# Spectral products over both parts in one pass, layer-norm sums taken while PSUM is emptied, and seven-product blocks in two more units

## The chip, the cores and the metric

The kernel runs on one core of one Trainium2 chip. The metric is the device time of one execution in microseconds (us); lower is better. One core has a matrix engine (TensorE; PE in the profile, with its weight loads as PEld), a vector engine (VectorE, DVE), a scalar engine (ScalarE, ACT), a general engine (GpSimd, POOL), and a queue engine (SyncE, SP) from which most DMA transfers are issued. Each engine takes its instructions in the order in which they were written, and waits where an operand is not ready or a buffer is still read.

## The reference, cut to what matters

Two layers of the same kind are applied to a sequence of S = 2048 tokens with D = 512 channels, in bf16. Each layer is a long convolution with gating and then a feed-forward network with F = 1792:

```python
def _A_ref(q, k, v, shift_k, ssm_k, ssm_D):
    kv = causal_shift_conv(k, shift_k) * v          # 4 taps
    y = irfft(rfft(pad(kv)) * rfft(pad(ssm_k)))[:S] # convolution along the sequence
    return q * (y + kv * ssm_D)
def _B_ref(x, w_gate, w_up, w_down):
    return (silu(x @ w_gate) * (x @ w_up)) @ w_down
x = A_q
x = x + _A_ref(_layernorm(x), A_k, A_v, ...)   # layer 0
x = x + _B_ref(_layernorm(x), ...)
x = x + _A_ref(_layernorm(x), A_k, A_v, ...)   # layer 1, same k, v, filters
x = x + _B_ref(_layernorm(x), ...)
```

Mean and variance of a layer norm run over the 512 channels of a token, with an epsilon of 1e-5. The convolution result does not depend on x, so it is computed once and used by both layers.

## The kernel before, in words

**Tiling.** The sequence is cut into four blocks c of 512 tokens, each held as 128 partitions by R = 4 rows by 512 channels. The convolution is done by blocks in the frequency domain: for every block the values X (from `kv`) and the filter H are transformed by matmuls with cosine and sine tables (`fwd`) and sums and differences on DVE (`m`, then X or H), the spectra are multiplied (`product`, which makes or adds to Z from X and G, where G is the spectrum of the filter), and Z is turned back by matmuls with `inv` (`inverse`) into Yk. A spectrum has four slots and two parts (real and imaginary), 512 channels each: 4096 elements per partition. Block c of the result needs the products of all pairs of blocks that sum to it, so Z is written by a first product and added to by later ones.

**Feed-forward units.** The network is done in 16 units (layer, c, h), each of two rows of a block (HP = 2, so 256 tokens). Their order is (0,0,0), (0,0,1), (1,0,0), (1,0,1), (0,1,0), (0,1,1), (1,1,0), (1,1,1), (0,2,0) and so on to (1,3,1). `prologue` (L926) stands ahead of each unit: the layer norm of x, the gate with Yk (`n`, then `xc<-xc,n`), the layer norm in front of the network, the normalised rows z, and their transposition by DMA into zT. `ffn` (L1085) takes the 14 tiles of F in groups of 4, 4, 4 and 2 (`GROUPS`). The gate and up products go to PSUM tiles pf; ACT applies silu (sg) and copies the up half (ht, hr); DVE multiplies. Units with ROWWISE groups (`by_rows`, L1060) have tokens on the partitions, so that `hr` has to be transposed by DMA into sg before the down product; their pf matmuls are 512 wide. The other groups have F on the partitions and 256-wide pf matmuls. The down product (L1159) is 512 wide, into the two PSUM tiles pd; ACT copies pd to dn (L1201), and DVE adds dn to x (L1204).

**Seven products.** In the units listed in `STRASSEN` (L31) the down product of a pair of F tiles, two token rows and two halves of D is done as a 2 x 2 block product with seven 256-wide matmuls instead of four of 512 (`seven`, L1004). That needs sums of weight blocks (wsa, wsb, wsc; `weight_sums`, L981, five passes of 1792 elements on DVE, once), sums and differences of the activations (cb, L1013 to L1017, three DVE operations for each group), four PSUM tiles per unit (two of the ring pd, two of pc), four copies out of PSUM on ACT (mt, L1046) and five sums on DVE (L1051 to L1058). Before, this is so for all groups of (0,3,0), (0,3,1), (1,3,0) and for two groups of (1,3,1).

**Statistics.** `ln_stats` (L851) takes mean and variance on DVE by `bn_stats` (L856) and `bn_aggr` (L857), adds epsilon (ve, L859), and has POOL take the power -1/2 (rstd, L861). `ln_stats_act` (L867) does it on ACT: a sum (jk with accumulation), a mean (nm), a sum of squares (jk, L881), ve (L885), and the same power on POOL (L887). `ST1` and `ST2` choose, for the first and the second layer norm, which units take which.

**Order.** Every operation is first recorded in a `Plan` by `add` with an engine, a cost and a delay; `Plan.order` (L200) then emits them in the sequence given by the table `ORDER`, a permutation of the recorded operations that was fixed ahead. Costs and delays decide which slot of a ring a buffer gets, and so what waits for what, but the sequence of instructions on each engine, SP's DMA issues among them, is that of the table. Buffers come from rings of fixed size: pf has four PSUM banks, pc and pd two each; s8 (ten slots of 8 KB per partition) holds spectra and larger intermediates, t4 (two slots of 4 KB) the partial products of `product`.

Of the kernel before, what the change touches and what calls it, by code (L numbers as in the profile page):

```python
# [9 lines left out]
P = 128  # L10
F32 = mybir.dt.float32
# [9 lines left out]
ST1 = lambda l, c, h: (l, c, h) in {(0, 0, 0), (0, 1, 0), (0, 2, 0), (0, 3, 0), (1, 0, 0)}  # L21
# [9 lines left out]
STRASSEN = {(0, 3, 0): 4, (0, 3, 1): 4, (1, 3, 0): 4, (1, 3, 1): 2}  # L31
# [88 lines left out]
]  # L120
R = 4

# [1346 lines left out]
```

## Time and profile before

| | before |
|---|---|
| median of 3 runs (lowest, highest) | 340.92 us (340.49, 341.29) |
| the profiled execution: its own time | 340.95 us |
| its span (first to last work on the engines) | 339.2 us |
| granted TensorE clock, mean | 0.998 |
| PE busy | 332.2 us, 98% |
| DVE busy | 305.4 us, 90% |
| ACT busy | 257.8 us, 76% |
| POOL busy | 41.1 us, 12% |

Times inside the profile are microseconds from the start of the span. A group line gives the line of the kernel, engine, operation, output and inputs by name and shape, the count, then the busy time of the group and the mean nanoseconds of one, then the idle time of that engine just before the group's instructions and what ended it. Consecutive matmuls overlap, so that the mean duration of one is longer than the distance from one start to the next.

### The profile page before, as it was taken

What the parts mean: (1) busy time and instruction counts of PE and PEld (TensorE: products, weight loads), DVE (VectorE), ACT (ScalarE), POOL (GpSimd) and SP (SyncE); (2) the same over time, 40 slices, a digit from 0 to 9 for tenths busy, and PEclk for the clock granted to TensorE, in tenths of its full rate; (3) what the DMA queues carried; (4) which work ended last, traced back from release to release, by engine and by line L of the source; (5) the groups of instructions that cost most, each with busy time, mean ns of one, the idle gap of its engine ahead of it and who ended that gap; (6) DMA issues with size and microseconds to landing.
All of it is one profiled execution on the core that took longest, in us unless ns stands there. A gap on an engine that the chain in (4) does not pass through costs nothing.

```text
span 339.2 us, 5867 instructions
## 1 busy us (share of the span) xinstructions
PE 332.2 (98%) x2119; PEld 201.9 (60%) x2151; DVE 305.4 (90%) x552; ACT 257.8 (76%) x514; POOL 41.1 (12%) x46
## 2 busy tenths in 40 slices
PE   8999999999999999999999999999999999999996
PEld 6647864644454564654445555645445487867884
DVE  7999999999999999999999999999999866987464
ACT  6899999988987467877899994869575465657463
POOL 4010110303110400103010200111201000100000
PEclk9999999999999999999999999999999999999999
DMA  7999403312643458341323245431414140213201
GB/s 287 322 312 354 59 15 79 62 31 48 140 108 77 98 123 161 75 111 31 63 48 77 46 80 129 115 37 32 89 11 94 28 92 2 49 47 73 55 0 64
DMA packets 77992, 31.59 MB, mean 93 GB/s; under 512 B 69765, under 2 KB 75786, under 8 KB 77962
## 3 DMA queue, kind: packets, MB, share of 16 engines
q1 hardware_dynamic: 77808, 31.13, 39.5%
q8 instruction: 17, 0.28, 0.4%
q14 instruction: 13, 0.11, 0.1%
q10 hardware_dynamic: 154, 0.07, 0.1%
HBM read 12.33 MB, written 2.10 MB: 43 GB/s over the span
## 4 chain that ended last, share of the span: by engine, by line
PE 83%; ACT 6%; DVE 5%; DMA 4%; issue 1%; POOL 1%; SPq 0%; ACTq 0%
PE pf L358 51%; PE pd L1159 18%; PE ps L358 6%; PE ps L1034 6%; DMA zT<-z 2%; DMA kn<-in_A_k_dram 1%; PE ps L844 1%; ACT H L466 1%; ACT X L466 1%; PE ps L505 1%; DVE bnst L856 1%; DVE m L587 1%; ACT jk L881 1%; ACT jk L875 1%; ACT hs L534 1%
## 5 line engine op out<-in xcount | busy, mean ns | idle before, releaser
L358 PEld LDWEIGHTS <-zT 128*128 128x128 bf16 x528 | 51.4, 98 | 61.1 <-DMA zT<-z 1.4
L358 PE MATMUL pf<-wu_sb,zT 128*128 128x512 bf16 x258 | 64.8, 379 | 0.4
L358 PE MATMUL pf<-wg_sb,zT 128*128 128x512 bf16 x256 | 63.6, 379 | 0.6 <-DMA zT<-z 0.3
L1159 PE MATMUL pd<-wd_sb,sg 128*128 128x512 bf16 x217 | 53.4, 379 | 0.5 <-DMA sg<-hr 0.2
L861 POOL TENSOR_TENSOR rstd<-ve,nhalf 128x2 f32<-128x2 f32 x24 | 27.9, 1165 | 206.4 <-DVE ve L859 206.4
L1072 ACT ACTIVATE sg<-pf 128x512 bf16<-128x512 f32 x66 | 38.9, 605 | 11.9 <-PE pf L358 11.4
L1073 ACT CAST hr<-pf 128x512 bf16<-128x512 f32 x66 | 38.5, 591 | 11.8 <-PE pf L358 11.0
L358 PE MATMUL pf<-zT,wg_sb 128*128 128x256 bf16 x368 | 46.7, 273 | 0.1
L358 PE MATMUL pf<-zT,wu_sb 128*128 128x256 bf16 x368 | 45.9, 273 | 0.0
L358 PEld LDWEIGHTS <-wg_sb 128*128 128x128 bf16 x368 | 35.9, 98 | 8.4
L358 PEld LDWEIGHTS <-wu_sb 128*128 128x128 bf16 x368 | 36.0, 98 | 7.3
L1159 PEld LDWEIGHTS <-sg 128*128 128x128 bf16 x224 | 21.7, 98 | 24.2 <-DMA sg<-hr 0.9
L1132 ACT ACTIVATE sg<-pf 128x512 bf16<-128x512 f32 x46 | 27.5, 608 | 8.1 <-PE pf L358 8.0
L856 DVE BATCH_NORM_STATS2 bnst<-xc 128x6 f32<-128x512 bf16 x48 | 31.4, 684 | 0.5
L1136 ACT CAST ht<-pf 128x512 bf16<-128x512 f32 x46 | 26.7, 591 | 5.7 <-PE pf L358 5.5
L1159 PE MATMUL pd<-wd_sb,ht 128*128 128x512 bf16 (+1 forms) x125 | 30.2, 369 | 0.3
L1139 DVE TENSOR_TENSOR ht<-ht,sg 128x512 bf16<-128x512 bf16 (+1 forms) x31 | 16.9, 548 | 8.5 <-ACT ht L1136 5.0
L700 DVE TENSOR_TENSOR t<-X,G 128x2048 bf16<-128x2048 bf16 x18 | 21.9, 1217 | 0.0
L704 DVE TENSOR_TENSOR t<-X,G 128x2048 bf16<-128x2048 bf16 x18 | 21.9, 1217 | 0.0
L1201 ACT CAST dn<-pd 128x512 bf16<-128x512 f32 x24 | 14.1, 594 | 10.2 <-PE pd L1159 7.6
L466 ACT ACTIVATE X<-ps 128x512 bf16<-128x512 f32 x32 | 19.1, 613 | 3.5 <-PE ps L358 3.1
L1079 DVE TENSOR_TENSOR hr<-hr,sg 128x1024 bf16<-128x1024 bf16 x27 | 18.5, 685 | 2.4 <-ACT hr L1073 1.6
(139 smaller groups left out, 506.8 us busy)
## 6 DMA issues: line engine op xcount, KB each, us to landing
hn<-in_A_ssm_k_dram SPq DMA_DIRECT2D x4, 512.0 KB, 3.9
vt<-in_A_v_dram SPq DMA_DIRECT2D x4, 512.0 KB, 6.5
xc<-in_A_q_dram SPq DMA_DIRECT2D x4, 512.0 KB, 6.2
out_dram<-xc SPq DMA_DIRECT2D x15, 128.0 KB, 1.8
wg_sb<-in_B_w_gate_dram SPq DMA_DIRECT2D x1, 1792.0 KB
wu_sb<-in_B_w_up_dram SPq DMA_DIRECT2D x1, 1792.0 KB, 7.5
wd_sb<-in_B_w_down_dram SPq DMA_DIRECT2D x1, 1280.0 KB, 11.2
sg<-hr SPq DMA_TRANSPOSE x66, 2.5
```

The costliest lines, as they stand in the source:

```text
L358: nc.tensor.matmul(o, lhsT=lhsT, rhs=rhs, start=(n == 0), stop=(n == len(terms) - 1))
L466: add("ACT", act(D), lambda: nc.scalar.activation(out=view(), in_=ps.t[:], func=ACT.Copy, scale=scale), r=[ps], w=[(buf, keys)], conv=conv)
L700: dve(n * D, lambda t1=t1, part=part: nc.vector.tensor_mul(out=t1.t[:], in0=x.t[:, sl, 0, :], in1=g.t[:, sl, part, :]), [(x, key(slots, (0 ...
L704: dve(n * D, lambda t2=t2, part=part: nc.vector.tensor_mul(out=t2.t[:], in0=x.t[:, sl, 1, :], in1=g.t[:, sl, 1 - part, :]), [(x, key(slots ...
L856: add("DVE", 0.6, lambda st=st, i=i: nc.vector.bn_stats(out=st.t[:], in_=xs[c].t[:, i, :]), r=[(xs[c], (i,))], w=[st])
L861: add("POOL", pw, lambda: nc.gpsimd.tensor_tensor(out=rstd.t[:], in0=ve.t[:], in1=nhalf.t[:].to_broadcast((P, n)), op=ALU.pow), r=[ve, nha ...
L1034: nc.tensor.matmul(bank.t[:, half_ * C:(half_ + 1) * C], lhsT=lhsT(i), rhs=rhs(i), start=(first and i == 0 and half_ == 0), stop=(last and ...
L1072: add("ACT", act(D), lambda ps=ps, dst=dst, o=o, which=which: nc.scalar.activation(out=rows(dst, o), in_=ps.t[:], func=ACT.Silu) if which ...
L1073: out=rows(dst, o), in_=ps.t[:], func=ACT.Silu) if which == "g" else nc.scalar.copy(out=rows(dst, o), in_=ps.t[:]),
L1132: add("ACT", act(D), lambda ps=ps, o=o, sg=sg: nc.scalar.activation(out=sg.t[:, o:o + 2, :], in_=ps.t[:], func=ACT.Silu), r=[ps], w=[(sg, ...
L1136: add("ACT", act(D), lambda ps=ps, o=o, ht=ht: nc.scalar.copy(out=ht.t[:, o:o + 2, :], in_=ps.t[:]), r=[ps], w=[(ht, (o // 2,))], due=(uni ...
L1159: nc.tensor.matmul((pds[o] if not cs.start else pds[HP]).t[:, cs], lhsT=ht.tiles(q, o), rhs=wt["d"].t[:, ft, cs], start=(ft == std0 and no ...
```

## The change

1. `product`: instead of a pass for each part (two multiplications of 2048 elements, one combination, and where Z exists an addition, for each of the two parts), X of one part is multiplied with both parts of G at once: two multiplications of 4096 elements, in which one operand is read with a repeated (stride 0) middle dimension; two combinations of 2048; and where Z exists one addition of 4096. The partial products t1 and t2 lie in s8 (eleven slots now); the ring t4 is gone.
2. Statistics: for the layer-1 norm of (1,1,0), (1,1,1), (1,2,0) and (1,2,1) the row sums come from ACT with the copy out of pd (`accum_out` on dn), added to the known mean of x from the norm before (`means`), and the squares from ACT; `bn_stats` and `bn_aggr` go away there. (1,0,0), whose sums ACT took in two passes of its own, gets them at the copy in the same way. In the other units epsilon is brought in by a constant triple (0, 0, 512 eps) that `bn_aggr` reads as a further set of statistics, so that the DVE operation for ve (L859) is gone and POOL reads the variance from mv itself.
3. `STRASSEN` has two more units, (1,2,0) and (1,2,1), all four groups; `weight_sums` is recorded ahead of (1,2,0).
4. X and Yk of block 3 use the PSUM ring pf instead of pc; the load of `w_down` is issued with its smaller part first; some estimated costs and delays of the `Plan` and its model of POOL are different; and the whole table `ORDER` is replaced, so that the sequence on all engines is new.

In the lists of instructions (before to after), PE has 56 matmuls of 512 columns fewer and 98 of 256 more; DVE has 554 instructions and then 526, ACT 487 and then 502, SP 152 in both, POOL two more (both settings of constants).

```diff
-ST1 = lambda l, c, h: (l, c, h) in {(0, 0, 0), (0, 1, 0), (0, 2, 0), (0, 3, 0), (1, 0, 0)}
+ST1 = lambda l, c, h: (l, c, h) in {(0, 0, 0), (0, 1, 0), (0, 2, 0), (0, 3, 0), (1, 0, 0), (1, 1, 0), (1, 1, 1), (1, 2, 0), (1, 2, 1)}
...
-STRASSEN = {(0, 3, 0): 4, (0, 3, 1): 4, (1, 3, 0): 4, (1, 3, 1): 2}
+STRASSEN={(1,2,0):4,(1,2,1):4,(0,3,0):4,(0,3,1):4,(1,3,0):4,(1,3,1):2}
+I_RING = lambda k: "pf" if k == 3 else "pc"
...
-        for part in (0, 1):
-            zk = (z, key(slots, (part,)))
-            t1 = new("t4", "t1", [P, n, D])
-            dve(n * D, lambda t1=t1, part=part: nc.vector.tensor_mul(out=t1.t[:], in0=x.t[:, sl, 0, :],
-                                                                     in1=g.t[:, sl, part, :]),
-                [(x, key(slots, (0,))), (g, key(slots, (part,)))], [t1], conv=conv)
-            t2 = new("t4", "t2", [P, n, D])
-            dve(n * D, lambda t2=t2, part=part: nc.vector.tensor_mul(out=t2.t[:], in0=x.t[:, sl, 1, :],
-                                                                     in1=g.t[:, sl, 1 - part, :]),
-                [(x, key(slots, (1,))), (g, key(slots, (1 - part,)))], [t2], conv=conv)
...
+        t1, t2 = new("s8", "t1", [P, R, 2, D], parts=2), new("s8", "t2", [P, R, 2, D], parts=2)
+        for t, part in ((t1, 0), (t2, 1)):
+            dve(8 * D, lambda t=t, part=part: nc.vector.tensor_mul(
+                out=t.t[:], in0=x.t[:, :, part:part + 1, :].to_broadcast((P, R, 2, D)), in1=g.t[:]), [(x, key(slots, (part,))), g], [t], conv=conv)
+        for part, comb in ((0, ALU.subtract), (1, ALU.add)):
+            out = z if first else t1
+            dve(4 * D, lambda part=part, comb=comb, out=out: nc.vector.tensor_tensor(
+                out=out.t[:, :, part], in0=t1.t[:, :, part], in1=t2.t[:, :, 1 - part], op=comb),
+                [(t1, (part,)), (t2, (1 - part,))], [(z, key(slots, (part,))) if first else (t1, (part,))], conv=conv)
+        if not first:
+            dve(8 * D, lambda: nc.vector.tensor_add(out=z.t[:], in0=z.t[:], in1=t1.t[:]), [t1], [z], conv=conv)
...
-        ve, rstd = new("ve", "ve", [P, n], F32), new("rs", "rstd", [P, n], F32)
-        add("DVE", 0.08, lambda: nc.vector.tensor_scalar(out=ve.t[:], in0=mv.t[:, :, 1], scalar1=LN_EPS, scalar2=None,
-                                                         op0=ALU.add), r=[mv], w=[ve])
...
+            st = plan.buf("bn", "bnst", lambda slot: bst.t[:, slot])
+            add("DVE", 0.6, lambda st=st, i=i: nc.vector.bn_stats(out=st.t[:, 0:6], in_=xs[c].t[:, i, :]), r=[(xs[c], (i,))], w=[st])
+            add("DVE", 0.09, lambda st=st, o=o: nc.vector.bn_aggr(out=mv.t[:, o, :], in_=st.t[:, 0:9]), r=[st, bst], w=[(mv, (o,))])
+        return mv, power(lambda: mv.t[:, :, 1], [mv], n, pw)
...
+            at, op = (lambda: prev.t[:, :, 0], ALU.subtract) if prev.name == "mv" else (lambda: prev.t[:], ALU.add)
+            add("DVE", 0.08, lambda: nc.vector.scalar_tensor_tensor(out=nm.t[:], in0=sm.t[:, 0:n], scalar=-1.0 / D, in1=at(), op0=ALU.mult, op1=op),
+                r=[(sm, range(n)), prev], w=[nm])
...
+                    add("ACT", act(D) + 0.14, lambda o=o: nc.scalar.activation(
+                        out=dn.t[:, o, :], in_=pds[o].t[:], func=ACT.Copy, accum_out=sm.t[:, o:o + 1]), r=[pds[o]], w=[(dn, (o,)), (sm, (o,))],
...
     def run(unit):
+        if unit in STRASSEN and not ws:
+            weight_sums()
         ffn(unit)
```

More of the change, by code (lines that the diff above doesn't have):

```diff
@@ L183, in add @@
                         b.readers[k].append(o)
-        o.two = eng == "DVE" and not any(b.ring in ("pf", "pc", "pd") or b.name == "bnst" for b in o.bufs)
-        o.late = 0
-        if eng == "POOL" and any(b.name == "rstd" for b in o.bufs):
-            o.late = 2 if any(q.eng == "ACT" and any(b.name == "ve" for b in q.bufs) for q in o.preds) else 4
+        o.two = eng == "DVE" and not any(b.ring in ("pf", "pc", "pd") or b.ring == "bn" for b in o.bufs)
+        o.late = int(eng == "POOL" and any(b.name == "rstd" for b in o.bufs))
         for b in o.bufs:
@@ L206, in order @@
         place, todo, free_at = {}, {}, {}
-        pend, gap, last = None, (0.0, 0.0), 0.0
+        pend, vec = None, []
         def settle(g):
-            pend.end = max(pend.start + pend.cost, max(g, pend.start) + pend.cost - 0.13)
+            pend.end = max(pend.start + pend.cost, g + pend.cost - 0.08)
             t["POOL"] = max(t["POOL"], pend.end)
@@ L229, in order @@
                     own[place[b]] = b
+            o.end = o.start + o.cost
             if o.eng == "DVE":
-                last = o.start
-                if pend is not None and pend.late == 4 and o.start + o.cost > pend.start:
-                    settle(0.0 if o.start >= pend.start - 0.02 else o.start + o.cost)
+                vec.append(o)
+                if pend is not None and (o.start >= pend.start + 0.08 or (o.two and o.end > pend.start)):
+                    settle(0.0 if o.start >= pend.start + 0.08 else o.end)
                     pend = None
-                g = (t["DVE"], o.start if o.two else o.start + o.cost)
-                if g[1] > g[0] + 0.05:
-                    gap = g
-                    if pend is not None and g[1] > pend.start + 0.03:
-                        settle(g[0])
-                        pend = None
-            o.end = o.start + o.cost
-            if o.late:
-                pend, t["POOL"] = o, o.end
-                if o.late == 4:
-                    if t["DVE"] > o.start:
-                        settle(t["DVE"] if last < o.start else 0.0)
-                        pend = None
-                elif gap[1] > o.start + 0.03:
-                    settle(gap[0])
+            if o.late:
+                pend, n = o, len(vec) - 1
+                while n >= 0 and vec[n].start >= o.start + 0.08:
+                    n -= 1
+                if n >= 0 and vec[n].two and vec[n].end > o.start:
+                    settle(vec[n].end)
                     pend = None
-            t[o.eng] = max(t[o.eng], o.end) if o.late else o.end
+                elif n < len(vec) - 1:
+                    settle(0.0)
+                    pend = None
+            t[o.eng] = max(t[o.eng], o.end)
             for b in o.bufs:
@@ L848, in inverse_half, with power @@
         evacuate_y(k, range(1, R))
+    def power(var, reads, n, cost):
+        rstd = new("rs", "rstd", [P, n], F32)
+        add("POOL", cost, lambda: nc.gpsimd.tensor_tensor(out=rstd.t[:], in0=var(), in1=nhalf.t[:].to_broadcast((P, n)), op=ALU.pow),
+            r=reads + [nhalf], w=[rstd])
+        return rstd
     def ln_stats(c, rows, pw=PW):
@@ L883, in ln_stats_act @@
                 r=[(xs[c], (i,)), nm], w=[jk, (sm, (n + o,))])
-        ve, rstd = new("ve", "ve", [P, n], F32), new("rs", "rstd", [P, n], F32)
+        ve = new("ve", "ve", [P, n], F32)
         add("ACT", TINY, lambda: nc.scalar.activation(out=ve.t[:], in_=sm.t[:, n:2 * n], func=ACT.Identity, scale=1.0 / D, bias=eps.t[:]),
             r=[(sm, range(n, 2 * n)), eps], w=[ve])
-        add("POOL", PWA, lambda: nc.gpsimd.tensor_tensor(out=rstd.t[:], in0=ve.t[:], in1=nhalf.t[:].to_broadcast((P, n)),
-                                                          op=ALU.pow), r=[ve, nhalf], w=[rstd])
-        return nm, rstd
+        return nm, power(lambda: ve.t[:], [ve], n, PWA)
     def shift_of(st, n, due=None):
@@ L1183, in ffn @@
             sm = None
-            if layer == 0 and ST1(1, c, h):
-                sm = sums[1, c, h] = new("st", "sm", [P, 2 * HP], F32, parts=2 * HP)
             for o in range(HP):
@@ L1199, in ffn @@
             dn = new("dn", "dn", [P, HP, D], parts=HP)
+            sm = None
+            if layer == 0 and ST1(1, c, h):
+                sm = new("st", "sm", [P, 2 * HP], F32, parts=2 * HP)
+                sums[1, c, h] = sm, means.pop((c, h))
             for o in range(HP):
-                add("ACT", act(D), lambda o=o: nc.scalar.copy(out=dn.t[:, o, :], in_=pds[o].t[:]), r=[pds[o]], w=[(dn, (o,))],
-                    due=(unit, 1.0, 3.0, "h"))
+                if sm is None:
+                    add("ACT", act(D), lambda o=o: nc.scalar.copy(out=dn.t[:, o, :], in_=pds[o].t[:]), r=[pds[o]], w=[(dn, (o,))],
+                        due=(unit, 1.0, 3.0, "h"))
+                else:
+                    add("ACT", act(D) + 0.14, lambda o=o: nc.scalar.activation(
+                        out=dn.t[:, o, :], in_=pds[o].t[:], func=ACT.Copy, accum_out=sm.t[:, o:o + 1]), r=[pds[o]], w=[(dn, (o,)), (sm, (o,))],
+                        due=(unit, 1.0, 3.0, "h"))
             sl = span(rows)
```

64 lines of the change are left out of this document (27 added, 37 removed), and 130 rows, old and new, of the table ORDER.

## The prediction, made before the run

> **What bounds the kernel now.** I read the summary and the chain of work first, then the group lines, then the timeline of PE (what a matmul costs, and where PE stands still), and last the windows of 20 us (which engine has room where).
>
> ```profile
> PE 332.2 (98%) x2119; PEld 201.9 (60%) x2151; DVE 305.4 (90%) x552; ACT 257.8 (76%) x514; POOL 41.1 (12%) x46
> PE 83%; ACT 6%; DVE 5%; DMA 4%; issue 1%; POOL 1%; SPq 0%; ACTq 0%
> ```
>
> PE carries the chain. The end therefore moves by two sums only: the work on PE, and the time in which PE stands still.
>
> ```profile
> 83.45 1.90 PE L1159 MATMUL pd<-wd_sb,sg 128*128 128x512 bf16 x8 [0.18 <-DMA sg<-hr]
> 85.19 1.04 PE L358 MATMUL pf<-zT,wg_sb 128*128 128x256 bf16 x8
> 86.06 1.03 PE L358 MATMUL ps<-Z,inv 128*128 128x512 bf16 x3
> ...
> 244.25 1.90 PE L358 MATMUL pf<-wg_sb,zT 128*128 128x512 bf16 x8 [0.28 <-DMA zT<-z]
> ...
> 282.59 1.26 PE L1034 MATMUL ps<-wsc,cb 128*128 128x256 bf16 x10
> 283.68 0.27 PE L1034 MATMUL ps<-wsa,cb 128*128 128x256 bf16 x1
> ```
>
> From start to start, eight matmuls of 512 columns take 85.19 − 83.45 = 1.74 us, eight of 256 take 0.87; over the whole trace the medians are 0.2159 and 0.1091 (and 0.0562 for 128). The ten of the seven-product code take 283.68 − 282.59 = 1.09: each has its own weight load and still costs 0.109. With the counts in the list of instructions, PE's work is 1006 × 0.2159 + 924 × 0.1091 + 217 × 0.0562 = 330.2 us. The span of 339.2 has 9.0 more: 3.3 before PE first runs without a break (at about 6 us), 1.23 in five gaps between 22 and 25 us (DVE and ACT have not finished the first spectra), 1.05 in all later gaps (the largest 0.44, at 244), and 3.4 from the last matmul to the end of the span.
>
> ```profile
> 160.00:180.00 20.00, 19.89 (x97) 9.42 (x97) 19.86 (x35) 16.99 (x32) 1.71 (x2) 1.00 0.30 59
> 180.00:200.00 20.00, 19.84 (x115) 11.41 (x117) 19.69 (x26) 19.43 (x40) 1.74 (x1) 1.00 0.29 59
> 200.00:220.00 20.00, 19.89 (x124) 12.12 (x124) 19.24 (x28) 13.83 (x28) 1.00 (x1) 1.00 0.46 114
> 220.00:240.00 20.00, 19.90 (x100) 9.77 (x101) 19.29 (x33) 17.13 (x40) 4.14 (x3) 1.00 0.28 46
> 240.00:260.00 20.00, 19.65 (x98) 9.53 (x99) 19.14 (x32) 12.50 (x24) 1.68 (x3) 1.00 0.37 58
> 260.00:280.00 20.00, 19.91 (x127) 12.42 (x128) 15.82 (x33) 10.12 (x18) 1.85 (x3) 1.00 0.31 62
> ```
>
> After window and length, the busy times are PE, PEld, DVE, ACT, POOL. DVE is as full as PE from 40 to 260 us: it idles 0.03 to 0.87 us in 20. PE does not stand still there only because DVE's results are ahead by some microseconds. After 260 DVE has 4 to 10 us of room in 20.
>
> **The change part by part.** Distances for DVE and ACT are again from start to start.
>
> ```profile
> L700 DVE TENSOR_TENSOR t<-X,G 128x2048 bf16<-128x2048 bf16 x18 | 21.9, 1217 | 0.0
> L714 DVE TENSOR_TENSOR Z<-Z,t 128x2048 bf16<-128x2048 bf16 x12 | 14.6, 1219 | 0.2
> L689 DVE TENSOR_TENSOR t<-X,G 128x1024 bf16<-128x1024 bf16 x8 | 5.3, 686 | 0.0
> L1051 DVE TENSOR_TENSOR xc<-xc,mt 128x1024 bf16<-128x1024 bf16 x4 | 2.8, 692 | 3.4 <-ACT mt L1046 3.3
> L856 DVE BATCH_NORM_STATS2 bnst<-xc 128x6 f32<-128x512 bf16 x48 | 31.4, 684 | 0.5
> L881 ACT ACTIVATE jk<-xc,nm 128x512 bf16<-128x512 bf16 x16 | 11.6, 724 | 0.2
> ```
>
> *Seven products in two more units (PE).* 56 × 0.2159 = 12.09 us go and 98 × 0.1091 = 10.69 come: −1.40 us. All of it is on the path, since PE is.
>
> The Trainium skill ("TensorE: Matmul & The Clock Gate", Back-to-back issue gap) says that in a stream of weight loads and matmuls one of 512 columns costs 131 ns and one of 128 costs 81. Between them 256 columns would be some 98 ns, an estimate, and this part would cost 98 × 0.098 − 56 × 0.131 = +2.3 us instead. The trace differs: 0.216 and 0.109 in just such streams, 282.59 included, and the measurement decides.
>
> *The same units on DVE and ACT.* cb, and the sums of mt: DVE gains 12 + 4 + 2 operations of 512 (0.335), 10 of 256 (0.202), 2 of 128 (0.14) and 4 of 1024 (0.602), less 2 additions of dn (0.602): +9.5 us. ACT gains 6 copies of 512 (0.48) and 2 of 256 (0.26) and loses 4 of dn: +1.5 us. In both engines all of it lies beside PE, as long as the engine is not late.
>
> *Products.* 36 multiplications of 2048 become 18 of 4096, 12 additions 6. From 1024 to 2048 a tensor operation grows from 0.602 to 1.136, so one of 4096 should take 1.136 + 2 × 0.534 = 2.20, and each pair saves some 0.07: 24 × 0.07 = −1.66 us on DVE. The 2048-wide subtractions and additions stay. One operand is repeated. L689 multiplies with one repeated already and L1051 adds with one: 686 and 692 ns, against 687 for plain 1024-wide ones (L1204). So I take the fast rate. The other bound is the rate of bn_stats, 512 elements in 0.605 us, about half as fast: +2.1 us for each of the 18.
>
> *Statistics.* DVE loses 8 bn_stats (0.605), 8 aggregations (0.118) and 24 ve (0.077), and gains 5 nm (0.1): −7.2 us. ACT gains 8 squares (0.76), 4 ve (0.2) and about 0.14 on each of ten copies, and loses two sums (0.62): with the copies of the seven products and small changes, its list grows from 243.8 to 252.6, +8.8 us. ACT has no full window but 20 to 60 and 180 to 200 (19.43), and it holds PE only through PSUM banks: counted along the two lists, no bank comes free later than PE wants it, in either version. I cost this at nothing; without that cover it is bounded by the 8.8. POOL's powers stay 32 (0.685 us at least, 1.165 in the mean, 4.13 at most). They end late when DVE runs two-input operations beside them: behind one of 4096 a power may end 1.07 us later than behind one of 2048, and the z behind it too; saved is the ve of 0.077 ahead of each. I take 0, bounds −0.1 and +1.1 for a z that PE is short of. The Trainium skill ("GPSIMD Engine Reference", Specifications) says that POOL shares its SBUF interfaces with VectorE, with contention when that has two SBUF inputs; the spread from 0.685 to 4.13 agrees, and by the rule the long products would make it wider.
>
> *SP.* It issues 152 in both, in a new order. sg<-hr and zT<-z take 2.5 us from issue to landing. t1 and t2 now share s8 with the loads of later blocks; a load whose slot is late would hold the transpositions behind it in SP's order. The slots grew by one, DMA is at 0.28 to 0.67 of its time; I take nothing, and a bound of one transposition, 2.5 us (in C).
>
> *DVE in all:* +9.5 −1.7 −7.2, with small terms: 0. But it moves. The five weight sums (1.08 us each) ran at 261 to 275 us, where DVE has room, and now run in 180 to 225 us; the cb of the two units, too, come at 235 to 265 instead of nothing.
>
> *Start, 22 to 25 us.* In the new sequence PE has 32 tap products ahead of the first use of m (m wanted after 21.8 us of PE's work, not 19.4), and DVE writes m no later. The 1.23 us go. What is late next: z for the first transpositions (ACT and DVE end it at 28.0 in both lists, PE wants it earlier now), which I put at 0.45; and in 40 to 65 us, where DVE idles 0.03 in 20 us, 0.5, since DVE's list up to the ht at 63 us of PE work grew by 0.7 us and its margin there was 0.8 and is 0.5. Bounds: 0 (its margins hold) and 1.23 (DVE sets the pace again).
>
> *SP, 78 to 90 us.* Two gaps of 0.34 and 0.27 (waits for sg and Z) before; the sequence is similar; 0.3.
>
> *DVE shortage at 232 to 256 us of PE work.* Here the change adds a wait: seven() of (1,2,0) wants its cb on DVE. The gate product whose silu DVE multiplies next ends at 213.2 us of PE's work; behind that multiplication DVE has, by the list, 18.9 us up to the end of the first cb: two 4096-wide (4.4), four of 2048 (4.6), ten of 1024 (6.0), and for the rest a weight sum, a bn_stats, small ones and normalisations. PE wants that cb at 232.2 to 232.7, 19.0 to 19.5 us later. With the 0.8 us from a matmul's end through ACT to DVE and the 0.3 back, as in the trace, DVE needs 20.0: at least 0.5 short. The Z for the block's inverse and three more cb come in the next 20 us at the same margin, with DVE gaps of 0.2 to 0.9 in 20 us as in the windows. Before, the same place had one wait of 0.44. I take 1.2; bounds 0.3 and 3.7 (every gap as in the worst window, and POOL's power at 4.1 ahead of one z). Past 256 the margin is over 13 us.
>
> *Sum.* Stalls before 1.23 + 1.05 = 2.28; after 0.45 + 0.5 + 0.3 + 1.2 = 2.45. The profiled execution took 340.95 (0.03 above the median, so both give the same): 340.95 − 1.40 + 0.17 = 339.7. I say 339.8.
>
> **The rivals.**
>
> A, the forecast: the PE work is saved, start and shortage cancel. 339.0 to 340.2.
>
> B, PE work and start are both kept: the cb and Z arrive in time and the stalls fall to 0.7 or so. 340.95 − 1.40 − 2.28 + 1.1 = 338.4. For it: DVE's sum is unchanged, and the lists are ordered to the same end as before. Against: DVE has no gap to give in 160 to 260.
>
> C, slower: DVE is late for the cb of (1,2,0) and (1,2,1). It decides when all stalls exceed 2.28 + 1.40 + 0.65 = 4.33 us, that is 2.0 more than I take, inside the bound of 3.7 for that one place. For it: five weight sums and two units' cb in full windows. 341.6 to 343.5; say 342.3.
>
> D, the same, with a shortage of 2 to 3: 340.3 to 341.6.
>
> E, the repeated operand runs at the slow rate: +2.1 us × 18 = 38 on an engine that has some 34 idle, most of it at the ends: about 370. L689 and L1051 speak against it.
>
> F, the new 256-wide matmuls do not hide their weight loads (98 ns in the records, under a distance of 109): from 14 ns shown on each of the 98 the gain is gone, from 18 the time is 341.6 and over; at 38, 343.5. The row at 282.59 speaks against it, where the same code hides them. The skill's figures named above come to this time.
>
> **How the numbers follow.** About 0.2% (0.68 us) is what a measurement can tell from no change: faster is under 340.24, slower over 341.6. A 0.38, B 0.17, C 0.21, D 0.20, E 0.03, F 0.01. Faster is A and B without a sliver: 0.54. Same is D with that sliver: 0.21. Slower is C, E, F: 0.25. The range leaves out E, half of C's far end and B's near end: 338.2 to 342.4; A's own is 339.0 to 340.2.
>
> **What would show it.** Right: 4096-wide products at 2.2 to 2.3 us; PE's busy time down by some 1.4 us; no gaps at ps<-m,inv near 22 to 25 us but one at the first transpositions; a PE wait for DVE cb or Z at 237 to 262 us of about a microsecond; DVE at 19.5 and more in 180 to 260. Wrong: gaps there of over 3 us (C), none (B), POOL's rstd holding z, or PE waiting for ACT copies of pd or mt, which I costed at nothing.

## The result, and the profile after

The changed kernel takes 343.40 us (median of 6 runs, 342.92 to 343.85) beside 341.12 us for the kernel before on the same chip (6 runs): a ratio of 1.0065, 95% interval 1.0049 to 1.0082. It is slower by 0.65%. The forecast was 339.8 with a range of 338.2 to 342.4, so the time lies outside the range and on the other side; it lies inside rival C (341.6 to 343.5), which had a chance of 0.21.

The profiled execution took 343.78 us with a span of 342.0; its summary and its chain of waits:

```profile
PE 331.7 (97%) x2162; PEld 205.5 (60%) x2193; DVE 303.8 (89%) x524; ACT 266.1 (78%) x545; POOL 37.6 (11%) x48
PE 70%; DVE 14%; DMA 6%; ACT 6%; issue 2%; POOL 2%; SPq 0%; DVEq 0%; ACTq 0%; POOLq 0%
```

PE's share of the chain has fallen from 83% to 70%, and DVE's has risen from 5% to 14%. The parts of the change did what they say: these group lines show the products of 4096 elements and the seven-product matmuls (1028 is line 1034 of the kernel before, 695 the multiplication of the products, 703 the last addition).

```profile
L695 DVE TENSOR_TENSOR t<-X,G 128x4096 bf16<-128x4096 bf16 x18 | 40.9, 2282 | 0.1
L703 DVE TENSOR_TENSOR Z<-Z,t 128x4096 bf16<-128x4096 bf16 x6 | 13.7, 2284 | 0.1
L1028 PE MATMUL ps<-wsc,cb 128*128 128x256 bf16 x78 | 11.3, 273 | 0.1
L1153 PE MATMUL pd<-wd_sb,sg 128*128 128x512 bf16 x171 | 42.3, 379 | 1.5 <-DMA sg<-hr 1.1
```

A product takes 2.28 us, 2.20 from start to start, as worked out; the seven-product matmuls stand 0.109 us apart in the new units as in the old. The windows of 20 us (length, then busy time of PE, PEld, DVE, ACT, POOL) show where PE lost time: 0.9 us at 80 to 100, 1.6 at 220 to 240, 1.4 at 300 to 320.

```profile
80.00:100.00 20.00, 19.07 (x97) 9.39 (x98) 16.01 (x33) 16.29 (x30) 2.25 (x3) 1.00 0.55 107
...
180.00:200.00 20.00, 19.89 (x113) 11.07 (x114) 19.38 (x24) 18.97 (x40) 4.12 (x1) 1.00 0.32 69
200.00:220.00 20.00, 19.80 (x118) 11.51 (x118) 19.41 (x22) 14.55 (x34) 1.97 (x1) 1.00 0.46 99
220.00:240.00 20.00, 18.38 (x90) 8.57 (x90) 19.79 (x29) 17.30 (x45) 2.38 (x3) 1.00 0.24 40
...
300.00:320.00 20.00, 18.64 (x140) 13.41 (x139) 14.08 (x37) 11.79 (x21) 1.39 (x2) 1.00 0.44 61
```

PE's timeline names what ended the waits (idle time before the line, and its releaser):

```profile
85.09 1.04 PE L1153 MATMUL pd<-wd_sb,sg 128*128 128x512 bf16 x4 [0.83 <-DMA sg<-hr]
...
232.88 1.02 PE L353 MATMUL pf<-wu_sb,zT 128*128 128x512 bf16 x4 [0.28 <-ACT sg L1066]
240.26 0.39 PE L1028 MATMUL ps<-wsa,sg 128*128 128x256 bf16 x2 [1.17 <-DMA sg<-hr]
...
302.43 1.67 PE L353 MATMUL pf<-wg_sb,zT 128*128 128x512 bf16 x7 [0.42 <-DMA zT<-z]
...
319.82 1.03 PE L353 MATMUL pf<-zT,wu_sb 128*128 128x256 bf16 x8 [0.93 <-DMA zT<-z]
```

Counted as the prediction counted them (how much more than usual lies from one matmul's start to the next; gaps under 0.12 us are left out, and so are holes of 0.21 to 0.22 us that nothing ended, where the record of one matmul is missing; "taken" is the value that the prediction took), PE's stalls after the first 6 us are:

| place, us | before | taken | after |
|---|---|---|---|
| 22 to 34 | 1.23 | 0.45 | 0.62 |
| 40 to 75 | 0 | 0.5 | 0.14 |
| 78 to 90 | 0.61 | 0.3 | 0.99 |
| 149 | 0 | 0 | 0.20 |
| 213 to 237 | 0 | 0 | 0.26 + 0.48 + 0.45 = 1.19 |
| 238 to 262 | 0.44 | 1.2 | 1.33 + 0.16 = 1.49 |
| 300 to 320 | 0 | 0 | 0.59 + 1.10 = 1.69 |
| sum | 2.28 | 2.45 | 6.32 |

The row 238 to 262 is the prediction's "232 to 256 us of PE's work": up to there PE had stood still for 3.3 us at the start and 3.1 us of stalls. 6.32 − 2.28 − 1.40 (PE's work) = +2.64 us; the two profiled executions differ by 343.78 − 340.95 = 2.83. So the saving on PE is there, and 4.0 us of new stalls take it back, in two places that need an explanation: 213 to 244 us, and the transpositions by DMA at 85, 302 and 320 us.

### The profile page after: what moved, and what is told of

The parts are those of the page before. It is cut to its first block, busy times and chain, and to the rows that moved or that the text cites. A ratio compares the mean times of both kernels' runs of the same rounds, so it can differ in the third digit from the quotient of the medians.

```text
span 342.0 us, 5971 instructions
## 1 busy us (share of the span) xinstructions
PE 331.7 (97%) x2162; PEld 205.5 (60%) x2193; DVE 303.8 (89%) x524; ACT 266.1 (78%) x545; POOL 37.6 (11%) x48
## 4 chain that ended last, share of the span: by engine, by line
PE 70%; DVE 14%; DMA 6%; ACT 6%; issue 2%; POOL 2%; SPq 0%; DVEq 0%; ACTq 0%; POOLq 0%
PE pf L353 43%; PE pd L1153 13%; PE ps L1028 6%; PE ps L353 5%; DMA zT<-z 2%; DMA sg<-hr 2%; PE ps L501 2%; POOL rstd L842 2%; DMA kn<-in_A_k_dram 1%; DVE m L583 1%; DVE t L695 1%; DVE t L699 1%; DVE bst L851 1%; DVE ka L651 1%; ACT jk L875 1%
## 5 line engine op out<-in xcount | busy, mean ns | idle before, releaser
L353 PE MATMUL pf<-wg_sb,zT 128*128 128x512 bf16 x259 | 65.0, 379 | 0.8 <-DMA zT<-z 0.4
L1153 PE MATMUL pd<-wd_sb,sg 128*128 128x512 bf16 x171 | 42.3, 379 | 1.5 <-DMA sg<-hr 1.1
L695 DVE TENSOR_TENSOR t<-X,G 128x4096 bf16<-128x4096 bf16 x18 | 40.9, 2282 | 0.1
L842 POOL TENSOR_TENSOR rstd<-mv,nhalf 128x2 f32<-128x2 f32 x20 | 16.6, 831 | 155.4 <-DVE mv L852 155.4
L842 POOL TENSOR_TENSOR rstd<-ve,nhalf 128x2 f32<-128x2 f32 x12 | 17.4, 1450 | 117.1 <-ACT ve L879 117.1
L1153 PEld LDWEIGHTS <-sg 128*128 128x128 bf16 x176 | 17.0, 98 | 21.0 <-DMA sg<-hr 2.3
L1153 PE MATMUL pd<-wd_sb,ht 128*128 128x512 bf16 (+1 forms) x119 | 28.4, 368 | 0.2
L851 DVE BATCH_NORM_STATS2 bst<-xc 128x6 f32<-128x512 bf16 x40 | 26.4, 683 | 0.4
L1028 PEld LDWEIGHTS <-cb 128*128 128x128 bf16 x195 | 19.0, 98 | 4.2 <-DVE cb L1007 0.3
L1040 ACT CAST mt<-ps 128x512 bf16<-128x512 f32 (+1 forms) x24 | 12.4, 536 | 10.6 <-PE ps L1028 10.4
```

The costliest lines, as they stand in the source:

```text
L353: nc.tensor.matmul(o, lhsT=lhsT, rhs=rhs, start=(n == 0), stop=(n == len(terms) - 1))
L695: dve(8 * D, lambda t=t, part=part: nc.vector.tensor_mul(out=t.t[:], in0=x.t[:, :, part:part + 1, :].to_broadcast((P, R, 2, D)), in1=g.t[: ...
L842: add("POOL", cost, lambda: nc.gpsimd.tensor_tensor(out=rstd.t[:], in0=var(), in1=nhalf.t[:].to_broadcast((P, n)), op=ALU.pow), r=reads + ...
L851: add("DVE", 0.6, lambda st=st, i=i: nc.vector.bn_stats(out=st.t[:, 0:6], in_=xs[c].t[:, i, :]), r=[(xs[c], (i,))], w=[st])
L1028: nc.tensor.matmul(bank.t[:, half_ * C:(half_ + 1) * C], lhsT=lhsT(i), rhs=rhs(i), start=(first and i == 0 and half_ == 0), stop=(last and ...
L1153: nc.tensor.matmul((pds[o] if not cs.start else pds[HP]).t[:, cs], lhsT=ht.tiles(q, o), rhs=wt["d"].t[:, ft, cs], start=(ft == std0 and no ...
```

## The experiments

Three theories were put against each other. Theory 1: DVE has no room between 160 and 245 us, and the weight sums and cb that the change puts there make PE wait. Theory 2: some DMA transpositions are late for a reason of their own, a fetch of PE instructions in flight (a transfer that brings the next block of PE's program). Theory 3 came up with the profile: the statistics on ACT made a new chain across engines. All ratios are to the kernel before, run on the same chip beside them; where runs come from different chips, a difference of ratios is the fairer comparison, and it is given beside the microseconds.

### The weight sums left out

```diff
-    tensor_tensor(out=out(), in0=x0(), in1=x1(), op=op)          # five of 1792 elements
+    tensor_tensor(out=out()[:, 0, 0:8], in0=x0()[:, 0, 0:8], in1=x1()[:, 0, 0:8], op=op)
```

> Leaves out the five weight sums on DVE (each becomes an operation of 8 elements; the seven products read unsummed weights). Theory 1 (DVE is short of time in 205 to 241 us, where two of the five lie): the PE stalls between 216 and 241 us, 2.8 us in the changed kernel, fall to 0.8 or less, and the time to 341.0 to 341.9. Theory 2 alone (late DMA transpositions at 85, 302 and 320 us cost the time): no more than 0.3 us below 343.4. Rival (long 4096-wide products hold DVE and POOL at the wrong places): 343.0 to 343.4.

Measured: 342.16 us, ratio 1.0035 (1.0021 to 1.0048): 1.2 us less than the changed kernel (1.0 by the ratios), less of a gain than theory 1 gave. The waits at 215, 223 and 232 us (1.19 together) are gone. The one before the first seven-product matmul of (1,2,0) is not; counted as in the table it is still 1.28 us:

```profile
239.59 0.61 PE L1028 MATMUL ps<-wd_sb,sg 128*128 128x256 bf16 x4 [1.12 <-DMA sg<-hr]
```

DVE now waits itself (0.91 for POOL's rstd at 216, 0.97 for the copies of pd on ACT at 229). From 228.6 us on it works without a gap of over 0.12 up to the multiplication of hr and sg that ends at 235.8; two transpositions follow, and the second lands at 239.54. So what PE waits for here is the length of DVE's list behind the down product before it, and work taken away ahead of that does not help. That is read from the order in this trace; no run tests it alone. Some 4.6 us of DVE work taken away (five times 1.00 less 0.07, from start to start) gave 1.2 back. The waits at 85 and 319 us stayed, as theory 2 needs.

### The weight sums early, in the kernel before

```diff
 # ORDER of the kernel before: the five weight sums on DVE
-    at 262 to 275 us
+    spread over 200 to 228 us
```

> The kernel before with one thing changed: its five weight sums on DVE go from 262 to 275 us, where DVE has room, to 200 to 225 us, about where the change puts them. Theory 1: DVE has under 0.8 us idle in 20 there, so PE waits 1 to 3 us more between 215 and 250 us: 342.0 to 344.0. If DVE's lead over PE is enough to take 5.2 us: 341.1.

Measured: 344.75 us, ratio 1.0107 (1.0091 to 1.0123), +3.6 us by this one move, 0.75 above what theory 1 gave at most. PE's timeline of this run:

```profile
207.34 0.81 PE L1093 MATMUL pd<-wd_sb,ht 128*128 128x512 bf16 x3 [0.57 <-DVE ht L1073]
210.85 1.04 PE L1093 MATMUL pd<-wd_sb,ht 128*128 128x512 bf16 x4 [0.97 <-DVE ht L1073]
221.94 0.38 PE L292 MATMUL ps<-vt,fwd 128*128 128x512 bf16 x1 [1.15 <-DVE vt L597]
225.59 1.04 PE L1093 MATMUL pd<-wd_sb,sg 128*128 128x512 bf16 x4 [0.47 <-DMA sg<-hr]
```

In the first three PE waits for DVE itself, in the very places in which the sums now lie; the fourth is for a transposition of 4.05 us that met a fetch of instructions (below). In the list of stalls these are 0.73, 1.13, 1.32 and 0.63 us, and two of 0.6 to 0.7 follow at 247 to 250, the second again behind a transposition of 4.04 us with a fetch in its flight. At 260 to 280 us, where the sums had been, DVE is busy 12.0 us of 20 and PE no less than before: the room there bought nothing. This settles theory 1 for the sums. (Placing them ahead of 180 us was not tried.)

### The two units' seven products taken back

```diff
-STRASSEN={(1,2,0):4,(1,2,1):4,(0,3,0):4,(0,3,1):4,(1,3,0):4,(1,3,1):2}
+STRASSEN={(0,3,0):4,(0,3,1):4,(1,3,0):4,(1,3,1):2}
 # the down products stand where the first seven-product matmuls of each group stood
```

> Units (1,2,0) and (1,2,1) get their ordinary 512-wide down products back, each placed where the first seven-product matmuls of its group stood; the weight sums stay where the change put them. Theory 1: PE works 1.40 us more and DVE some 9.5 less; the stalls of 232 to 241 us shrink, those of 216 to 224 (0.9) and the DMA ones stay: 342.2 to 343.6. If the two units pay what they save on PE without any cost: 344.8.

Measured: 343.49 us, ratio 1.0064 (1.0047 to 1.0081): no difference from the changed kernel. PE works 1.40 us more, and its stalls, counted as in the table, are 5.0 us instead of 6.3: at 240 us it waits 0.45 instead of 1.33 + 0.16, and the waits at 302 and 320 us are gone, but those at 85 (1.55) and 279 (0.83) are longer or new. The waits at 215, 223 and 233 us (1.2) are still there, for the weight sums are.

### Both taken back

```diff
 # as above, and the five weight sums on DVE
-    at 184 to 227 us
+    at 253 to 273 us, ahead of multiplications for which DVE idles there
```

> The changed kernel without the third part of the change: units (1,2,0) and (1,2,1) get their 512-wide down products back, as in the run without the two seven-product units, and the five weight sums go behind 250 us, where DVE idles in that run. Theory 1 (DVE has no room for sums and cb in 180 to 245 us): the waits of 0.25, 0.5, 0.45 and 0.45 us between 214 and 241 go, 1.2 to 1.7 us together: 341.7 to 342.5; what is left over the kernel before is the transposition at 84 us (1.0 to 1.5). If the sums cost nothing where they are: 343.4.

Measured: 342.11 us, ratio 1.0029 (1.0017 to 1.0041). The waits of 213 to 244 us are down to 0.41. Against the changed kernel this is 1.2 us less (1.0065 − 1.0029), with 1.40 us more work on PE: the third part of the change costs 1.2 us where it was to gain 1.4. The run has waits of its own, 0.83 at 277 us (the run above has it at 279) and 0.30 at 282, so the third part may cost more than that. What is left, the first two parts in the new sequence, is still 0.9 us slower than the kernel before, although DVE has 9.3 us less to do (296.1 us busy, from 305.4). Its stalls are 3.0 us, from 2.28 before; the 0.83 and 0.57 at 85 us are the largest of them. No run has the first two parts in the old sequence, so what the new sequence by itself costs stays open.

### The other DVE savings undone one at a time

```diff
 # products: each 4096-wide multiplication or addition, in its place
-    tensor_mul(out=t[:], in0=x[:, :, part:part+1].to_broadcast(...), in1=g[:])
+    [tensor_mul(out=t[:, :, j], in0=x[:, :, part], in1=g[:, :, j]) for j in (0, 1)]
```

> Every multiplication and every last addition of 4096 elements of the spectral products is issued as two of 2048, in the same place; the result is the same. Theory 1: DVE has 24 times some 0.07 us more to do, 0.4 us of it in 205 to 241 us: 343.4 to 344.4. Rival (the 4096-wide ones are what makes it slow, through POOL's power waiting behind them or a slower rate): 342.0 to 343.0.

Measured: 344.75 us, ratio 1.0102 (1.0083 to 1.0120): +1.35 us (1.3 by the ratios) for the 1.66 us that DVE has more to do. The rival falls. Where the time arises is not shown: the profiled execution took 344.20 us, only 0.42 more than that of the changed kernel, and its stalls are 6.2 us, no more than there.

```diff
-ST1: ... (1, 1, 0), (1, 1, 1), (1, 2, 0), (1, 2, 1)
+ST1: ... none of these four; bn_stats and bn_aggr at the place of nm
```

> The four units' statistics go back to DVE (bn_stats and bn_aggr at the place of nm; the copies of pd without sums). Theory 1 (DVE's amount of work is what is short): DVE has 1.3 us more in each of the four, 2.6 of it in 205 to 241 us: 344.5 to 346.5. Theory 3 (the statistics on ACT made a new chain: nm on DVE, then two squares on ACT, behind which the copies of gate and up products of (1,2,0) wait, and with them the multiplication, its transposition and PE): the wait of 1.3 us at 239 us shrinks to under 0.7, and the time is 342.3 to 343.6.

Measured: 348.83 us, ratio 1.0212 (1.0179 to 1.0244): +5.4 us (5.0 by the ratios), for 8 × 0.605 + 8 × 0.118 − 4 × 0.1 = 5.4 us of DVE work. Without the chain over ACT the wait ahead of the first seven products is 2.26 us (counted as in the table), not less:

```profile
245.91 0.39 PE L962 MATMUL ps<-wsa,sg 128*128 128x256 bf16 x2 [2.09 <-DMA sg<-hr]
```

So theory 3 does not carry the loss. What the chain costs by itself this run cannot tell, since it takes the chain away and adds DVE work in the same place. Theory 1 had the sign but was too small, since it counted only the two units at 205 to 241 us; new waits come from 145 to 245 us, wherever the statistics stand.

### The urgent multiplication first

```diff
 # near 230 us, order on two engines
-ACT:  square, square, ve, ve | sg, sg, hr, hr, hr        DVE: n, n, n*Yk, xc+n, hr*sg, X, X
+ACT:  sg, sg, hr, hr, hr | square, square, ve, ve        DVE: hr*sg, X, X, n, n, n*Yk, xc+n
```

> The changed kernel with a few instructions moved near 230 us, nothing else: on ACT the two squares and ve of the norm of (1,2,1) (and what follows them) go behind the copies of the first gate and up products of (1,2,0), and on DVE the multiplication of these goes ahead of that norm's n. Theory 3: the multiplication is some 2 us earlier, the waits at 232 (0.45) and 239 us (1.3) shrink to under 0.5 together, and the time is 341.7 to 342.5, unless the z that now comes later shows up as a new wait. Theory 1 alone: DVE is no less busy, 343.0 to 343.6.

Measured: 347.93 us, ratio 1.0187 (1.0157 to 1.0217), 4.5 us slower than the changed kernel (4.2 by the ratios): both expectations missed. In the changed kernel the copies sg do stand behind the two squares on ACT, which wait for nm on DVE:

```profile
230.17 0.72 ACT L875 ACTIVATE jk<-xc,nm 128x512 bf16<-128x512 bf16 x1 [0.40 <-DVE nm L871]
...
232.25 1.06 ACT L1066 ACTIVATE sg<-pf 128x512 bf16<-128x512 f32 x2
```

With them ahead, PE's wait for sg before the first seven products is nearly gone (0.19), but the next is 3.1 us:

```profile
243.40 0.61 PE L962 MATMUL ps<-wd_sb,cb 128*128 128x256 bf16 x4 [3.08 <-DVE cb L941]
```

DVE's timeline of this run shows why:

```profile
235.22 0.69 DVE L1007 TENSOR_TENSOR hr<-hr,sg 128x1024 bf16<-128x1024 bf16 x1 [1.29 <-ACT hr L1001]
235.83 1.29 DVE L534 TENSOR_TENSOR X<-m 128x1024 bf16<-128x1024 bf16 x2
237.94 0.73 DVE L837 TENSOR_SCALAR n<-xc,nm,rstd 128x512 bf16<-128x512 bf16 x2 [0.83 <-POOL rstd L776]
...
240.72 2.28 DVE L629 TENSOR_TENSOR t<-X,G 128x4096 bf16<-128x4096 bf16 x1
242.92 0.42 DVE L941 TENSOR_TENSOR cb<-sg 128x512 bf16<-128x512 bf16 x1
```

The multiplication now waits for its copies on ACT and the norm for its statistics; DVE stands still for 2.1 us, and cb comes 2.5 us later than in the changed kernel (240.39). So at 230 to 240 us DVE's amount and the chain from ACT bind together, and moving one operation ahead only delays another.

### The fetches of instructions

In the profiles a queue that carries instructions (q8) moves 16 KB about every 20 us, 17 times for the 4,355 matmuls and weight loads that the profile of the changed kernel has. Theory 2 was tested by changing only how many warm-up matmuls PE issues ahead of the work, which shifts the places of all later fetches: the one at 80.5 us in the changed kernel comes at 76.2 with 66 more instructions of PE ahead, at 84.2 with 33 fewer and at 86.9 with 50 fewer. So it is PE's queue. The answer of the trace on the DMA queues between 315.6 and 319.7 us of the changed kernel (queue, packets, MB, share) shows one in flight, with a transposition that takes 4.1 us:

```profile
q8 instruction: 1, 0.02, 1.5%
issues: line engine op xcount, KB each, median us to landing
zT<-z SPq DMA_TRANSPOSE x1, 4.1
```

and the chain of waits in the same stretch shows PE waiting for it:

```profile
315.62 4.06 DMA zT<-z
319.68 0.14 issue
319.82 1.25 PE pf L353 x10
```

At 85 us two things met. The transposition that PE waits for there took 4.77 us, from 80.27 to 85.04, and in its stretch lie a fetch and half a megabyte of a load (q1 carries transpositions and loads):

```profile
q1 hardware_dynamic: 1622, 0.79, 86.6%
q8 instruction: 1, 0.02, 2.2%
```

```diff
-    for _ in range(n):      matmul(t[:], rhs=ones)                       # 128 columns
+    for _ in range(2 * n):  matmul(t[:, 0:64], rhs=ones[:, 0:64])
```

> The warm-up matmuls at the very start are doubled in number and halved in width, so that PE has some 66 more instructions ahead of the work; nothing else differs. Theory 2 (a fetch of PE instructions in flight, 16 KB about every 20 us, lengthens a DMA transposition from 2.5 to 3.1 to 4.8 us, and PE waits for three such at 85, 302 and 320 us): the fetches come about 5 us earlier, these three waits (0.9, 0.4 and 0.9 us) go or shrink, others may come up elsewhere: 341.3 to 342.6. Theory 1 alone: 343.2 to 343.7, and the three waits stay where they were.

Measured: 347.78 us, ratio 1.0193 (1.0174 to 1.0213). The three waits did not stay: those at 85 and 302 us are gone, and at 320 us PE waits for another tile. But others came, 0.87 at 125, 0.85 at 147 and 1.80 at 247 us among them (counted as in the table, as all waits of this part), and together they are larger; that the time would fall was wrong. 1.6 us of the loss is a late start: PE waits at 23 us for kTb, whose transposition took 7.33 us with a fetch at 21.2 in its flight, and 5.0 to 6.1 in the other 13 profiles, where none met it. The waits at 125, 147 and 247 stand behind transpositions of 3.79, 4.47 and 4.23 us with a fetch in their flight. The one that had landed at 85 us met the load alone and took 4.00, and PE did not wait for it.

```diff
+    for _ in range(n // 2): matmul(t[:], rhs=ones twice)                 # 256 columns
```

> The warm-up matmuls are halved in number and doubled in width, so that the same start takes some 33 PE instructions fewer (the run with more of them also began late, which this one should not). Theory 2: PE's instruction fetches come about 2.5 to 3 us later; those that met the transpositions landing at 302 and 320 us pass behind them, and these waits (0.6 and 1.1 us) go; the one at 84 us (1.0) may stay, since the fetch moves into the same group of transpositions: 341.5 to 342.5. If fetches have nothing to do with it: 343.2 to 343.7.

Measured: 343.08 us, ratio 1.0051 (1.0036 to 1.0067). In the chain of waits of this run nothing but PE is left where the changed kernel waited at 320 us:

```profile
311.96 2.73 PE pf L353 x25
314.69 4.54 PE ps L1028 x40
319.23 2.84 PE pf L353 x26
```

The wait at 85 us is 0.38 at 88; the one at 302 is longer, 0.87, for the fetch at 300.8 now meets that transposition in the middle (4.0 us). The expected gain was too large, since this wait was to go too; the intervals of this run and of the changed kernel overlap, so the time alone does not tell them apart.

```diff
+    for _ in range(n // 4): matmul(t[:], rhs=ones four times)            # 512 columns
```

> The changed kernel with a quarter of the warm-up matmuls at four times the width (some 50 PE instructions fewer ahead of the work). Theory 2: fetches come about 4 us later than in the changed kernel; of the waits at 84 (1.0), 302 (0.6) and 319 us (1.1) at least two go, and one or two of the same kind may come up elsewhere: 341.8 to 343.2. Without fetches: 343.2 to 343.7.

Measured: 345.31 us, ratio 1.0118 (1.0104 to 1.0131), above the expected span. The waits at 85 and 320 us are gone, as theory 2 said of two; but 1.98 us came at 64 (a transposition of 4.45 us from 59.74, with a fetch at 60.97), 0.80 at 90, and the one at 302 grew to 1.32.

The halving (256 columns) in the kernel before:

> The same halving of the warm-up matmuls in the kernel before. Theory 2: its waits of 0.34 at 83 us and 0.44 at 244 us, both behind transpositions that a fetch met, move or go, and others may appear: between 340.2 and 342.5, and any new PE wait of over 0.4 us lies behind a transposition of over 3 us with a fetch in its flight. If fetches have nothing to do with it: 340.8 to 341.2 with the waits where they were.

Measured: 341.82 us beside 341.11, ratio 0.9999 (0.9974 to 1.0023). (The two medians are 0.2% apart; among the 23 runs of the kernel before beside this one, two took 343.77 and 345.36.) The waits at 83 and 244 us fell from 0.34 and 0.44 to under 0.12 and 0.17; one at 91 us grew from 0.27 to 1.39, behind a transposition of 4.55 us that met a load of half a megabyte, not a fetch. So the kernel before is not free of this either, and the expectation for new waits, that a fetch stands behind each, is missed: this one stands behind a long transposition, but a load made it long.

And in the kernel without the third part of the change:

> The same kernel with the warm-up matmuls halved in number and doubled in width (33 PE instructions fewer ahead). Theory 2: the fetch that meets the transposition landing at 85 us moves, and this wait falls from 1.0 to 1.5 us to about 0.4, as it did in the changed kernel: 340.8 to 341.9, at or under the kernel before. Without it: the same time as the run above.

Measured: 342.22 us, ratio 1.0026 (1.0017 to 1.0034), the same as without, and not the gain that theory 2 gave: the wait at 85 us (0.57) went to 88 (0.42), and one of 0.78 came at 63, behind a transposition of 3.25 us that met a fetch.

Over all 14 profiles, after the first 50 us, the trace gives the landing of 986 transpositions sg<-hr and zT<-z. Put in groups by the packets that overlap them in time (a fetch is a packet of 16 or 8 KB on a queue of instructions, a load or store a packet of 512 bytes or more):

| in flight beside it | count | median, us | longest, us | over 2.75 us |
|---|---|---|---|---|
| neither | 608 | 2.44 | 2.54 | 0 |
| a fetch of 16 KB (PE), with or without others | 162 | 3.61 | 5.45 | 122 |
| a fetch of 8 KB alone | 101 | 2.46 | 3.53 | 20 |
| a load or store alone, of 0.2 MB or more | 39 | 3.87 | 4.55 | 32 |

The other 76 had smaller loads, or a load and a fetch of 8 KB, beside them. So theory 2 had one of two causes: a large load lengthens a transposition as a fetch does. At 302 and 320 us of the changed kernel only a fetch was there (3.90 and 4.06 us). At 85 us it was both. In the four runs with shifted fetches of the changed kernel, with or without its third part, the load made that transposition 3.7 to 4.0 us long, without a wait of PE over 0.12 (in one of them a fetch began 0.1 us before the landing). In the seven runs of it with load and fetch together it took 4.40 to 5.45 us, with waits of 0.42 to 1.55. The wait at 223 us, too, is for a transposition that met a fetch (3.62 us), although it goes when the weight sums are left out. Of the times that theory 2 gave for shifted fetches none came true in the changed kernel, with or without its third part: the waits moved, and as many came as went. No row shows what of the DMA hardware they share; that fetch and load are the cause rests on these counts and on the waits that moved with the fetches.

## Why the prediction was wrong

**What bounds, PE's work, the prices.** Right. PE's work fell by 1.40 us at 0.216 and 0.109 us a matmul (no sign of rival F, and the figure of 131 ns that the Trainium skill has in "TensorE: Matmul & The Clock Gate", Back-to-back issue gap, holds in neither kernel). The 4096-wide operations take 2.20 us (no rival E). DVE's sum fell by 1.6 us in busy time, near the 0 that was worked out. Rival F's 343.5 lies beside the measured time by chance only, since the cost that it needs is not there.

**Start, 22 to 25 us.** Right in kind and nearly in size: the five gaps went, and 0.62 came at 30 to 34 us, where 0.45 was taken; of the 0.5 taken for 40 to 65 us only 0.14 came.

**"But it moves": a term put at nothing.** The price of "DVE shortage at 232 to 256 us" was nearly right at its own place: 1.2 taken, 1.49 measured, and its sign, a wait of about a microsecond at 237 to 262 us, came. (PE waited for the transposition of sg, one step ahead of the cb that was counted.) What failed is that the count began at 213.2 us of PE's work, as if DVE were on time there and nothing lay ahead. The five weight sums, moved to 184 to 227 us, got no price; 1.19 us came at 215, 223 and 232, which go when the sums are left out, and the same move in the kernel before costs 3.6 us.

**"DVE in all: 0" as a reason for calm.** DVE's sum decides nothing where its windows are full. 5.4 us more DVE work cost 5.4 us, 1.66 cost 1.35, 5.0 moved there cost 3.6; but 4.6 less gave back 1.2. In a stretch where DVE and PE are both at 19 to 20 us of 20, added work was paid for at 0.7 to 1.0 of its length in these runs, and relief was soon caught by the next wait.

**"ACT ... I cost this at nothing".** Nearly right as to the bank waits (0.26 and 0.45 us at 215 and 232.9 in the table's count, both gone without the weight sums, so DVE's lateness is behind them). Not seen: squares on ACT wait for nm, which is now on DVE, and the copies for the multiplication stand behind them, as ACT's timeline at 230 us shows. What that costs alone stays open: the run that turned the order round lost more on the other side. POOL's powers, taken at 0, are right: 32 of them took 34.0 us, 37.5 before, and the longest 4.12, 4.13 before, so the longer products did not draw them out.

**"sg<-hr and zT<-z take 2.5 us", and with it "SP, 78 to 90 us ... 0.3" and nothing for 300 to 320.** This is the step with the largest miss: 0.99 and 1.69 us came, 2.4 more than taken. 2.5 us holds for a transposition with nothing else in flight (2.44). With a fetch or a large load beside it the median is 3.6 to 3.9, and the two gaps of before, which the prediction carried over as waits for sg and Z, were already such: the transpositions behind them took 4.18 and 4.19 us. Which ones are met depends on how many instructions PE has issued by then, which any change on PE moves, and on where the loads lie.

Together with the small differences at 22 to 75 us and the 0.20 at 149 us, these terms make up the miss: stalls of 2.45 were taken and 6.32 came, 3.87 more, while the profiled time came out 4.1 above the sum.

**The chances.** C's time was right (341.6 to 343.5), and the range cut off half of it. Its reason, "five weight sums and two units' cb in full windows", is half of what happened: without the 2.4 us behind long transpositions the stalls would have been 3.9 by the same count, under the 4.33 from which C decides, and the time 341.2, which is rival D. That the measured time lies in C is in part luck. (Two slips of the working change nothing here: B lets the stalls fall to 0.7 and adds 1.1, and 4.33 is 1.9 more than was taken, not 2.0.)

## What to carry to other kernels

Where two engines are both full, price each operation moved into that stretch at its full length and start the count of slack where the engine was last seen waiting, not at a point where it is assumed to be on time. A saving of 1.4 us on the bounding engine was not worth 9.5 us of new and 5 us of moved work on its neighbour in the one stretch where the neighbour has no room. Where short DMA transpositions lie on the path, look at what else is in flight beside each, and leave slack behind them (here 1.2 us in the median for those met by a fetch, 3.0 at most). Otherwise expect the time to move with any change in the instruction count (by −0.3, +1.9 and +4.4 us in three shifts of the changed kernel), and judge a small change only over several such shifts.

## What the runs showed of the hardware

A fetch of 16 KB of PE instructions lengthened a DMA transposition in flight from 2.44 to 3.61 us in the median, and a load of 0.2 MB or more to 3.87 (above). PE was not seen to wait for its own instructions: every wait after 40 us in the table of stalls was ended by another engine or by a transfer of data. The Trainium skill ("Runtime: NRT & Kernel Launch", Instruction fetch mechanics) says that an engine refills in blocks of 16 KB, 256 instructions, and that the cost is mostly hidden; the count of 17 agrees (17 × 256 = 4,352), and for the fetching engine so does the cost, but not for the transpositions.

The stall of over 3 us in the run with the urgent multiplication first had a price beyond itself. The window behind it shows the granted clock at 0.63 (the figure after POOL's count):

```profile
244.00:248.00 4.00, 3.52 (x16) 2.05 (x15) 3.16 (x5) 2.58 (x6) 0.69 (x1) 0.63 0.22 44
248.00:252.00 4.00, 3.95 (x22) 2.14 (x21) 3.97 (x7) 1.67 (x3) 0.00 (x0) 0.95 0.74 90
```

and its matmuls of 256 columns stood 0.21 us apart instead of 0.109: some 1.7 us lost in these 8 us (4 × 0.37 + 4 × 0.05). With some 2.4 us more of stalls than the changed kernel, that is nearly all of the 4.5 us that this run lost to it. No stall of the changed kernel itself (1.33 us at most) moved the clock, nor did the one of 2.26 us in the run with the statistics back.
